# Gated mix of a diagonal state-space layer and a Hedgehog linear attention: loads on one queue, a numerators' factor in four copies, a new step list

## The chip, the cores and the metric

The kernel runs on one core of a Trainium2 chip. The metric is the device time of one execution in microseconds (us), lower is better; the figure for a kernel is the median of several executions.

The engines that matter here: PE (matrix products; its weight loads are listed as PEld), DVE (vector engine), ACT (scalar engine, also activations), POOL (GpSimd) and SP, which issues DMAs. ACT issues DMAs too, in line with its other work; these rows carry the name ACTq, those of SP the name SPq. Each engine takes its own instructions in the order in which the program lists them, and waits at the first whose inputs are not there.

## What is computed

With x of 2048 rows by 512 columns in bf16, the reference is a gated sum of two branches:

```python
g = sigmoid((x * gate_w).sum(-1, keepdims=True))
# branch a: diagonal complex state space
h = Lam_bar * h + B_bar @ x[t]           # for t in 0..2047, 512 complex states
a = 2.0 * real(C @ h) + x * Dskip
# branch b: linear attention, 32 heads of 16
q, k, v = split(x @ wqkv)
phi(y) = concat(softmax(y @ w_phi), softmax(-(y @ w_phi)))
num = phi(q) @ (phi(k).T @ v);  den = phi(q) @ phi(k).sum(0) + 1e-6
b = (num / den) @ wo
out = g * a + (1 - g) * b
```

## The kernel before, in words

**Tiles.** x is cut into 16 tiles of 128 rows. Tile `ti` holds rows of one residue modulo 4 (`ti // 4` is the residue); `x_load` (L224) brings it in by one DMA transpose, so that `xT` holds x with the columns on the partitions. The keys and values are worked on in the order of the tiles, queries and outputs in the order `order` (L259): residues 3, 1, 0, 2.

**Start.** ACT issues the two halves of the key weights into `wk_nat` (L161; the trace calls this buffer C2r), SP the small `w_phi` (L162) and then the transposes of x tiles 0 to 7 (L232). PE runs a row of products that only keep it busy (`F:n`, L802, tile `spin`). `st_W` (L263) transposes a quarter of the key weights on PE, and the copy out of PSUM (`evac`, L113: L115 on ACT, L117 on DVE when the step has `:D`) fills `WTk` (in the trace: Xq). `fold` (L397) multiplies it by the block diagonal of `w_phi`, and the copy fills `Wk2` (in the trace: Wk). From then on `st_k` (L446) makes the projected keys of a tile and `st_v` (L453) its values, four products each (L444) and one copy to SBUF. `st_V` (L299) transposes the state-space parameters on PE and copies them to `vec` (L303); `st_U`, `st_P`, `st_P2` to `st_P4` and `st_i` (L315 to L427) make powers, angles and the tables of sines and cosines out of them, on DVE and ACT.

**Middle.** For a group of two or four tiles `feat_max`, `feat_min`, `feat_exp`, `feat_sum` (L485 to L533) make the two softmaxes: a maximum and a minimum by a tree of DVE operations (L480), two differences (L490, L496), exponentials on ACT (L134), sums by a tree, then a normalising product on DVE (L517 for keys, L528 for the tiles whose features are transposed). `st_a` adds the keys' products with the values into PSUM. `st_p`, `st_g`, `st_z`, `st_h` and `st_K` are the state space in blocks of four time steps: input products, the scan (L616), and the products that bring the states back.

**End.** For a group of four output tiles the normalised query features are transposed by DMA (`phT`, L532). `st_o` (L729) multiplies them by the keys' sums (`pn`, L740), takes the logarithm of the denominators (`ld`) and copies the numerators (`nu`), makes the reciprocal factor `rd` on ACT (L746) and the product `on` on DVE (L748), and transposes it by DMA into `oT` (L753). `st_y` (L708) has put the state-space branch into PSUM; `st_t` (L756) adds `oT` times `wo` (L760), scales by the gate (`ot`, L764 on ACT, L766 on DVE) and writes the tile out (L768).

**What sets the order.** Every piece of work is a generator, and `ORDER` (L24) is a list of tokens. Each token runs one piece of one generator up to its next `yield`; `@3` names the PSUM banks that it takes, `:D` puts a copy on DVE, `:A` an output on ACT's DMA queue. The schedule of PE, DVE, ACT and SP is exactly this order (`manual_schedule`, L150). Tokens of interest: `l8` to `l15` load x tiles, `LV` (L295) loads V's weights, `NR` and `NI` (L275) load the real and imaginary part of B as it lies, `R0` to `R3` and `I0` to `I3` (L279) load B transposed, `O` loads `wo`. A DMA gets one of eight completion semaphores in turn, and waits at its issue for the transfer that had that semaphore before. So `LV` on ACT waits for the first BrT transpose on SP.

The three lines that read the numerators' factor:

```python
aexp(out=rd[:], in_=ld[:], func=ACT.Exp, scale=-1.0, bias=nge[:, ti:ti + 1])
VT(out=on[:]..., in0=nu[:]...,
   in1=rd[:].rearrange("p a h -> p (a h)").unsqueeze(2).to_broadcast([P, 32, Dh]), op=ALU.mult)
```

Of the kernel before, what the change touches and what calls it, by code (L numbers as in the profile page):

```python
# [23 lines left out]
ORDER = """  # L24
B R0 R3 R2 F:40 l8 W0@0 W1@1 W1:D W2@2 W2:D l9 W3@3 W3:D f1@4 W0 f0@5 f0:D LV f2@6 f1 f3@0 f3:D f2 k0@1 k0 NR V@2 V U
P k1@3 U U U P P2 P2 P2 NI k3@4 P R1 P2 P2 P4 k1 P4 k2@5 P4 i3 i3 P2 i3 i3 i0 P3 i0 P3 F:6 V2@6 V2 i3 v3@0 v3 n0 i2
k5@1 k5 k2 i0 k3 i0:D M n0 n0 i1 v4@2 v4 k6@3 k6 n0 l12 l11 v7@6 x0 x0 x0 i1 i1 x0 x0 x1 k4@0 v5@1 k4 i0 i2 i2 i1:D i1
i2:D k7@5 v0@4 p0:D p0:D p0 p0 p1:D p1:D v1@2 v2@3 F:6 n0 x1 x1 x1 k7 i2 x1 x2 v9@0 x2 x2 n1 v5 n1 x2 L p1 l10 v2 e0
I3 n1 n1 e0 n1 v1 v6@5 v0 gw p0:D v6 g100@1 p0:D n2 n2 s0 p1 p1:D v8@7 l15 s0 s0 s0 g000@3 v7 k8@2 l13 D g000 n2 l14
e1 s0 s0 Q0 e1 s0 s1 k8 p0 s1 s1 k9@4 k10@5 p1 g000 g100 g100 k9 k10 a0@62 a0 v9 v10@3 s1 s1 s1 x2 v8 k11@1 p2 k11 n2  # L30
I2 n2 s1 k13@4 k13 g010@5 g010 e2 e2 e2 p1 e2 a1 a1 x3 x3 I0 k12@0 x3 x3 x3 v10 k14@7 I1 k15@1 g011@4 k14 g001@3
g101@7 n3 p0 k15 n3 n3 k12 n3 n3 g001 s2 s2 s2 s2 v11@1 x4 x4 x4 n4 n4 n4 p1 p2 e3 Q1 e3 g001 s2 s2 s2 g011 p3 g011 e3
n4 p3 p3 g101 p2 e3 s3 v11 Q2 g011 g010 g010 g110@0 g110 Q3 w3@3 a2 a2 a2 w1@1 s3 w1 p3 a2 p2 g101 w0@4 w0 g111@5 g111
g111 C0 s3 s3 x4 s3 C5 z0 s3 p3 g110 g111 g110 w2@1 z0 z0 p3 g200@7 g200 w2 w3 q2@4 q3@5 x4 n4 e4 e4 q2 C6 p3 z0 s3
q0@0 q0 z1 g200 g300@1 z1 z1 z1 C4 z1 e4 e4 s4 p2 p2 s4 v14@3 v14 g300 g300 g211@4 z1 z1 c02 q1@0 q1 v15@7 p3 c02 p2
z0 v12@3 z0 z0 s4 g301@1 q15@0 q3 C2 c02 C3 q15 c11 c11 a3 g201@5 c11 v13@0 v13 z1 a3 v12 v15 a3 a3 c13 p2 g210@0 s4
s4 s4 C7 c13 xA z1 c00 q5@3 g201 g201 q5 g311@7 nA z1 s4 z0 z0 g210 c01 c01 c01 xA xA z0 c12 c12 c12 g210 g210 c13
g211 g211 g211 z2 g301 q14@5 xA g301 h00@3 z2 h00 g310@0 C1 h01@4 nA nA q14 c00 g311 g311 c03 c03 h11@1 g311 q9@5 g310
g310 a4 a4 a4 a4 xA nA c03 c00 nA z2 z2 q8@3 c10 c10 r1 h11 q9 eA c10 q10@7 Y z2 eA eA eA r1 Y q8 z2 g310 z2 q4@5 h01
q10 q6@1 sA sA z3 z3 q12@6 h10@3 G q7@4 sA sA z3 q7 q4 q12 sA K3@0 z2 K3 y3@7 sA K2@4 z2 z3 z2 h21@5 y2@6 sA sA O  # L40
q13@0 q13 h10 sA Y Y q6 h20@3 K1@2 K1 r0 r0 z3 K0@0 z3 z3 z3 sA K0 z3 z3 h31@1 h30@2 b0 sA sA h20 h30 h31 h21 y2 y2
END X1 X1 N1 N1 N1 N1 o3@0 X1 o1@3 o2@5 X1 X1 o1 o3 o3@2 o3 o3 q11@1 o3 o2 o2@3 y3 q11 y6@0 o1@2 y0@5 N1 b1 o2 b1 o1
o1 G X2 X2 o2 o1 y3 y6 N2 E1 G G o2 N2 E1 E1 y1@1 E1 o3 o0@3 X2 o0 y0 K2 y7@2 y7 N2 y1 S1 S1 S1 o1 o0@3 o0 X2 S1 X2 y0
o2 y7 t3 S1 o0 o0 r3 S1 r3 y1 o0 S1 N2 N2 t3 t3 t1 S1 t1 E2 E2 b3 y6 b0 y5@4 r2 y5 r2 t2 y4@3 y4 y4 t2 S1 y5 S1 S1 E2
t0 t0 y14@7 E2 S1 b3 b2 y10@1 X3 b2 y10 X3 X3 X3 o5@6 o5 o5@5 o5 o5 y14 o6@6 X3 o6 o6@5 S2 o5 o5 S2 y14 S2 S2 o6 o6 o6
N3 N3 o4@6 o4 o4@5 o4 o4 y10 o7@6 y8@5 y8 S2 S2 o7 o7@6 o4 N3 y8 N3 S2 t0 o7 y11@6 S2 o6 o7 N3 E3 t6 o7 t6:D t5 o4 t4
E3 E3 E3 y11 t5:D t4:D S2 o8@0 o8 o8@4 o8:D o8 y15@3 S2 y15 S3 o9@4 o9 S2 o7 o8 S2 S3 S3 o9@0 o9 o9 y15 S3 o10@4 o9
t4:A o10:D o10@0 o8 o10 o9 S3 t7 o10 y9@0 y9 t7 y13@4 S3 S3 o10 y9 o10 o11@2 S3 S3 S3 t8 S3 o11 o11@2 o11:D o11 o11 t9
y12@2 y12 t8 t8:A t1:A t9:D t9:A o12@5 o12 o12@0 y11 o12:D o12 o12 o11 t2:A t6:A o13@5 o13:D t7:A o13@0 o13:D o13 t10
o13 o14@5 o14:D y13 o14@0 S3 o14:D o14 t11 o14 t10 o12 o13 o15@5 o15:D o15@0 o14 o15:D o15 o15 y12 t12 t12 y13 t13  # L50
t11:D t11:A t12:A o15 t10 t5 t14 t15 t13 t14 t14 t15 t13 t15:A
"""
# [14 lines left out]
def kernel(  # L67
# [65 lines left out]
    def aexp(**kw):  # L133
        ins = nc.scalar.activation(**kw)  # L134
# [159 lines left out]

    def st_LV():  # L295
        nc.scalar.dma_start(out=Wv[:], in_=B_wqkv[:, 2 * D:3 * D].rearrange("(k p) n -> p k n", p=P))
# [432 lines left out]
    def st_o(n):  # L729
        ti = order[n]  # L730
        op_ = pools["op"][1]
        ph = phT0[:, n] if n < 4 else live["ph", n // 4][:, n % 4]
# [15 lines left out]
        VT(out=on[:].rearrange("p g h e -> p (g h) e"), in0=nu[:].rearrange("p a h e -> p (a h) e"),  # L748
           in1=rd[:].rearrange("p a h -> p (a h)").unsqueeze(2).to_broadcast([P, 32, Dh]), op=ALU.mult)
# [3 lines left out]
        nc.sync.dma_start_transpose(out=oT[:], in_=on[:].rearrange("p g h e -> p (g h e)"))  # L753
# [84 lines left out]
```

## Time and profile before

| what | value |
|---|---|
| median of 3 executions | 187.26 us (186.46 to 188.04) |
| the profiled execution, its own time | 188.37 us |
| its span, first to last instruction | 186.6 us |
| mean granted clock of PE over the span | 0.982 |
| DVE, ACT busy | 151.8 us, 126.8 us |
| bytes moved by DMA | 16.99 MB |

A row of a timeline gives start and length in us, the engine, the line, the operation, the tile written and the tiles read, and in brackets the idle time before it and who ended that. A row of the groups gives a count, the total and the mean duration in ns. For a DMA the row is the issue on its queue; the landing time is listed apart.

### The profile page before, as it was taken

What the parts mean: (1) busy time and instruction counts of PE and PEld (TensorE: products, weight loads), DVE (VectorE), ACT (ScalarE), POOL (GpSimd) and SP (SyncE); (2) the same over time, 40 slices, a digit from 0 to 9 for tenths busy, and PEclk for the clock granted to TensorE, in tenths of its full rate; (3) what the DMA queues carried; (4) which work ended last, traced back from release to release, by engine and by line L of the source; (5) the groups of instructions that cost most, each with busy time, mean ns of one, the idle gap of its engine ahead of it and who ended that gap; (6) DMA issues with size and microseconds to landing.
All of it is one profiled execution on the core that took longest, in us unless ns stands there. A gap on an engine that the chain in (4) does not pass through costs nothing. (4 is left out here: it accounts for less than half of the span.)

```text
span 186.6 us, 2958 instructions
## 1 busy us (share of the span) xinstructions
PE 158.2 (85%) x1049; PEld 78.9 (42%) x1068; DVE 151.8 (81%) x306; ACT 126.8 (68%) x258; POOL 9.9 (5%) x28
## 2 busy tenths in 40 slices
...
GB/s 146 112 111 185 171 182 2 84 84 111 77 99 0 11 89 101 56 39 100 62 2 4 0 0 167 59 31 28 28 97 179 86 104 168 107 100 233 174 168 85
DMA packets 55198, 16.99 MB, mean 91 GB/s; under 512 B 50576, under 2 KB 55184, under 8 KB 55184
## 3 DMA queue, kind: packets, MB, share of 16 engines
...
q8 instruction: 8, 0.13, 0.3%
q14 instruction: 6, 0.05, 0.1%
...
## 5 line engine op out<-in xcount | busy, mean ns | idle before, releaser
L444 PEld LDWEIGHTS <-xT 128*128 128x128 bf16 x192 | 18.6, 99 | 32.3 <-issue 12.9
L444 PE MATMUL pk<-Wk,xT 128*128 128x512 bf16 x62 | 17.3, 410 | 9.0 <-ACT Wk L115 7.0
L134 ACT ACTIVATE EEk<-EEk 128x1024 bf16<-128x1024 bf16 x20 | 20.1, 1055 | 0.5 <-DVE EEk L496 0.5
L760 PE MATMUL py<-Wo,oT 128*128 128x512 bf16 x62 | 15.7, 379 | 2.8 <-DMA oT<-on 2.7
L583 PE MATMUL pgq<-xT,LBT 128*128 128x512 bf16 x62 | 16.2, 379 | 0.1
L444 PE MATMUL pq<-Wq,xT 128*128 128x512 bf16 x62 | 15.6, 379 | 0.6 <-ACT Wq L115 0.2
L444 PE MATMUL pv<-Wv,xT 128*128 128x512 bf16 x63 | 15.7, 379 | 0.1
L134 ACT ACTIVATE EEq<-EEq 128x1024 bf16<-128x1024 bf16 x12 | 11.9, 1045 | 4.0 <-DVE EEq L496 4.0
L134 ACT ACTIVATE ld<-pn 128x16 f32<-128x16 f32 x32 | 5.9, 189 | 12.2 <-PE pn L740 11.5
L717 PE MATMUL py<-Wk,H 128*128 128x512 bf16 x32 | 12.1, 378 | 0.9 <-ACT nu L115 0.6
L717 PE MATMUL py<-C2r,H 128*128 128x512 bf16 x32 | 12.1, 379 | 0.2
L718 PE MATMUL py<-Wv,H 128*128 128x512 bf16 x30 | 11.3, 378 | 1.0 <-DVE Wv L679 1.0
L115 ACT CAST Xq<-pq 128x512 bf16<-128x512 f32 x16 | 9.0, 591 | 3.9 <-PE pq L444 3.9
L748 DVE TENSOR_TENSOR on<-nu,rd 128x512 bf16<-128x512 bf16 x16 | 10.9, 684 | 0.5
L718 PE MATMUL py<-C2i,H 128*128 128x512 bf16 x29 | 11.0, 379 | 0.0
L740 PE MATMUL pn<-KVm,phT 128*128 128x68 bf16 x128 | 7.4, 195 | 4.1 <-DMA phT<-EEq 3.3
L740 PEld LDWEIGHTS <-phT 128*128 128x128 bf16 x128 | 6.1, 97 | 10.5 <-DMA phT<-EEq 6.6
L117 DVE CAST nu<-pn 128x256 bf16<-128x256 f32 x10 | 4.1, 422 | 7.9 <-ACT ld L134 7.9
L717 PEld LDWEIGHTS <-H 128*128 128x128 bf16 x64 | 6.2, 98 | 8.3 <-issue 2.1
L115 ACT CAST Xq<-pk 128x512 bf16<-128x512 f32 x16 | 9.0, 600 | 1.1 <-PE pk L444 1.1
L764 ACT ACTIVATE ot<-py,G 128x512 bf16<-128x512 f32 x11 | 7.3, 675 | 3.4 <-PE py L760 3.4
L616 DVE TENSOR_TENSOR_SCAN w<-ssm_par,ut 128x512 bf16<-128x512 f32 x8 | 9.5, 1214 | 0.0
(180 smaller groups left out, 357.1 us busy)
## 6 DMA issues: line engine op xcount, KB each, us to landing
...
Wv<-in_B_wqkv_dram ACTq DMA_DIRECT2D x1, 512.0 KB, 4.5
Bn_r<-in_A_B_re_dram ACTq DMA_DIRECT2D x1, 512.0 KB, 6.9
Bn_i<-in_A_B_im_dram ACTq DMA_DIRECT2D x1, 512.0 KB, 5.2
Wo<-in_B_wo_dram SPq DMA_DIRECT2D x1, 512.0 KB, 4.0
xT<-in_A_x_dram SPq DMA_TRANSPOSE x16, 3.2
```

Source lines behind the costliest of these rows:

```text
L115: nc.scalar.copy(out=out_ap, in_=in_ap)
L117: nc.vector.tensor_copy(out=out_ap, in_=in_ap)
L134: ins = nc.scalar.activation(**kw)
L444: MM(out=pt[:], lhsT=xT[:, kt, ti * P:(ti + 1) * P], rhs=W[:, kt, :], start=(kt == 0), stop=(kt == KT - 1))
L583: MM(out=pgq[:], lhsT=LBT_[:, kt, js], rhs=xT[:, kt, (r1 - 1) * NC:r1 * NC], start=False, stop=(r1 == 1 and kt == KT - 1))
L616: nc.vector.tensor_tensor_scan(out=w[:, ri, :], data0=rb, data1=ut[:, ri, :], initial=0.0, op0=ALU.mult, op1=ALU.add)
L717: MM(out=py[:], lhsT=src[:, j, 0, off:off + P], rhs=cr[:, j, :], start=(j == 0), stop=False)
L718: MM(out=py[:], lhsT=src[:, j, 1, off:off + P], rhs=ci[:, j, :], start=False, stop=False)
L740: MM(out=pn[:, 4 * m:4 * m + 4, :].rearrange("p h e -> p (h e)"), lhsT=ph[:, 4 * hf + m, :], rhs=KVm[:, 4 * hf + m, :], start=(m == 0), st ...
L748: VT(out=on[:].rearrange("p g h e -> p (g h) e"), in0=nu[:].rearrange("p a h e -> p (a h) e"), in1=rd[:].rearrange("p a h -> p (a h)").uns ...
L760: MM(out=py[:], lhsT=oT[:, g, :], rhs=Wo[:, g, :], start=False, stop=(g == HG - 1))
L764: nc.scalar.mul(out=ot[:], in_=py[:], mul=G[:, ti:ti + 1])
```

## The change

The diff does four things. The loads of V's weights, `Bn_r` and `Bn_i` move from ACT's DMA queue to SP's; V's is issued behind the first four x tiles instead of at a token. The factor `rd` is written four times over, side by side, so that the product reads it in runs of four (before, each value is read with a step of 0 over 16). The list `ORDER` is written anew, and the tokens `LV` are gone; its makers counted the time from one operation of an engine to a dependent one of the same engine. The fills are 36, 6 and 6 instead of 40, 6 and 6.

```diff
-    for ti in range(8):
+    for ti in range(4):
+        x_load(ti)
+    nc.sync.dma_start(out=Wv[:], in_=B_wqkv[:, 2 * D:3 * D].rearrange("(k p) n -> p k n", p=P))
+    for ti in range(4, 8):
         x_load(ti)
...
     def st_N(ri):
-        nc.scalar.dma_start(out=(Bn_r, Bn_i)[ri][:], in_=(A_B_re, A_B_im)[ri].rearrange("(j p) d -> p j d", p=P))
+        nc.sync.dma_start(out=(Bn_r, Bn_i)[ri][:], in_=(A_B_re, A_B_im)[ri].rearrange("(j p) d -> p j d", p=P))
...
-    def st_LV():
-        nc.scalar.dma_start(out=Wv[:], in_=B_wqkv[:, 2 * D:3 * D].rearrange("(k p) n -> p k n", p=P))
-        yield
...
-        rd = op_.tile([P, 2, 16], BF16, name="rd")
+        rd = op_.tile([P, 32, 4], BF16, name="rd")
...
-        aexp(out=rd[:], in_=ld[:], func=ACT.Exp, scale=-1.0, bias=nge[:, ti:ti + 1])
-        yield
-        VT(out=on[:].rearrange("p g h e -> p (g h) e"), in0=nu[:].rearrange("p a h e -> p (a h) e"),
-           in1=rd[:].rearrange("p a h -> p (a h)").unsqueeze(2).to_broadcast([P, 32, Dh]), op=ALU.mult)
+        aexp(out=rd[:], in_=ld[:].rearrange("p a h -> p (a h)").unsqueeze(2).to_broadcast([P, 32, 4]), func=ACT.Exp, scale=-1.0, bias=nge[:, ti:ti + 1])
+        yield
+        VT(out=on[:].rearrange("p g h (a b) -> p (g h) a b", b=4), in0=nu[:].rearrange("p c h (a b) -> p (c h) a b", b=4),
+           in1=rd[:].unsqueeze(2).to_broadcast([P, 32, Dh // 4, 4]), op=ALU.mult)
```

The list's first and last tokens, old and new (the whole list is 27 lines):

```diff
-B R0 R3 R2 F:40 l8 W0@0 W1@1 W1:D W2@2 W2:D l9 W3@3 W3:D f1@4 W0 f0@5 f0:D LV f2@6 f1 f3@0 f3:D f2 k0@1 k0 NR V@2 V U
-P k1@3 U U U P P2 P2 P2 NI k3@4 P R1 P2 P2 P4 k1 P4 k2@5 P4 i3 i3 P2 i3 i3 i0 P3 i0 P3 F:6 V2@6 V2 i3 v3@0 v3 n0 i2
+NR F:36 W1@0 W0@1 W0 B F:6 l10 W3@2 W2@3 W1 f0@4 f0 l15 W3:D f3@5 f3 W2:D f1@6 f1:D f2@1 f2 V@2 V P U P P2 P2 NI l9 U
+l8 P P2 P2 k1@0 U R1 k1 P2 P4 l12 U V2@3 P4 k2@4 V2 P2 k2 P4 P3 P3 i0 i2 k0@5 k0 i0 i2 i3 l11 k3@6 k3 i2 R0 n0 v2@1 i0
...
-o13 o14@5 o14:D y13 o14@0 S3 o14:D o14 t11 o14 t10 o12 o13 o15@5 o15:D o15@0 o14 o15:D o15 o15 y12 t12 t12 y13 t13
-t11:D t11:A t12:A o15 t10 t5 t14 t15 t13 t14 t14 t15 t13 t15:A
+o13 o14 o15@5 o15 y15@4 o14 o14 o15@3 o15 o15 o15 o15 y15 t8:A t11 t11:D t11 t12 t12 t9 t13 t9:A t13:D t13 t14 t14 y15
+t12 t14:A t15 t15 t15:A
```

In this new order SP issues, after the small load: x0 to x3, V's weights, x4 to x7, Bn_r, x10, x15, Bn_i, x9, x8, a BrT transpose, x12, x11, two of BrT, x13, the last of BrT, x14. ACT's first work after its two loads and the table load is the copies of W0, W1, f0, f3 and f2; DVE copies W3, W2 and f1. Of the nu copies DVE makes 4 (10 before), of the output scalings 3 (5 before), of the Bn scalings 6 (7 before).

More of the change, by code (lines that the diff above doesn't have):

```diff
@@ L24 @@
 ORDER = """
-B R0 R3 R2 F:40 l8 W0@0 W1@1 W1:D W2@2 W2:D l9 W3@3 W3:D f1@4 W0 f0@5 f0:D LV f2@6 f1 f3@0 f3:D f2 k0@1 k0 NR V@2 V U
-P k1@3 U U U P P2 P2 P2 NI k3@4 P R1 P2 P2 P4 k1 P4 k2@5 P4 i3 i3 P2 i3 i3 i0 P3 i0 P3 F:6 V2@6 V2 i3 v3@0 v3 n0 i2
-k5@1 k5 k2 i0 k3 i0:D M n0 n0 i1 v4@2 v4 k6@3 k6 n0 l12 l11 v7@6 x0 x0 x0 i1 i1 x0 x0 x1 k4@0 v5@1 k4 i0 i2 i2 i1:D i1
-i2:D k7@5 v0@4 p0:D p0:D p0 p0 p1:D p1:D v1@2 v2@3 F:6 n0 x1 x1 x1 k7 i2 x1 x2 v9@0 x2 x2 n1 v5 n1 x2 L p1 l10 v2 e0
-I3 n1 n1 e0 n1 v1 v6@5 v0 gw p0:D v6 g100@1 p0:D n2 n2 s0 p1 p1:D v8@7 l15 s0 s0 s0 g000@3 v7 k8@2 l13 D g000 n2 l14
@@ L30 @@
[L30 to L49, printed above, removed]
@@ L50 @@
-o13 o14@5 o14:D y13 o14@0 S3 o14:D o14 t11 o14 t10 o12 o13 o15@5 o15:D o15@0 o14 o15:D o15 o15 y12 t12 t12 y13 t13
-t11:D t11:A t12:A o15 t10 t5 t14 t15 t13 t14 t14 t15 t13 t15:A
+NR F:36 W1@0 W0@1 W0 B F:6 l10 W3@2 W2@3 W1 f0@4 f0 l15 W3:D f3@5 f3 W2:D f1@6 f1:D f2@1 f2 V@2 V P U P P2 P2 NI l9 U
+l8 P P2 P2 k1@0 U R1 k1 P2 P4 l12 U V2@3 P4 k2@4 V2 P2 k2 P4 P3 P3 i0 i2 k0@5 k0 i0 i2 i3 l11 k3@6 k3 i2 R0 n0 v2@1 i0
+i0:D i3 i0 i3 i3 x0 n0 v4@2 k4@0 v4 x0 R2 n0 k6@3 x0 i1 n0 x0 i1 i3 k5@4 k5 i1 l13 v6@5 x0 i1:D i1 v7@6 x1 R3 n0 x1 n1
@@ new lines @@
+x1 gw i2:D M D p1:D l14 x1 v3@2 v1@4 p0:D p0:D k6 n1 p1:D n1 v6 k4 p0 n1 k7@3 i2 L x1 e0 p0 p0:D n1 e0 v3 s0 k7 p1 p1
+v0@5 n2 v1 e1 v0 x2 k8@0 F:6 s0 I1 x2 s0 e1 v7 x2 s0 s0 s0 v5@7 k10@2 k10 k15@3 v5 p0:D n2 k12@4 s1 k9@5 k9 s0 k8
+k11@6 v9@2 n2 k11 s1 k12 x2 s1 n2 a0@75 a0 s1 s1 s1 I2 x2 I0 n2 x3 g100@0 k13@6 v2 k15 p1 p1 s1 k13 e2 x3 g010@4 p1
+g010 e2 e2 e2 I3 g100 x3 k14@1 k14 n3 x3 n3 p0 a1 a1 p3 v9 g000@3 g000 n3 p0 v10@6 g111@1 g100 p2 g001@2 x3 s2 g001 x4
+Q3 Q0 g000 s2 n3 s2 x4 p3 s2 n3 g011@0 g011 g001 p2 p1 s2 Q2 x4 s2 e3 C2 n4 g010 g011 g011 p2 g110@3 g110 Q1 e3 g010
@@ new lines @@
+e3 g101@2 g101 n4 g111 g101 e3 g111 x4 w3@0 s2 w1@4 z0 z0 p3 w2@2 w2 g110 g110 z0 z0 z0 a2 p2 w3 a2 a2 a2 n4 w1 O s3
+v13@2 n4 g111 p3 p3 C3 w0@3 w0 s3 x4 s3 v8@0 z1 z1 s3 v10 v8 p2 p2 z0 v13 v12@4 p3 q2@1 p2 p2 C4 z1 q3@3 v12 n4 z0 z0
+q0@6 q3 q0 q1@0 g200@2 s3 q1 q2 e4 e4 e4 g301@4 nA z1 z1 z1 v11@3 s3 v11 q5@6 p3 g210@0 s3 xA g210 g201@1 z0 e4 s4 z0
+v14@3 g201 g201 nA g200 a3 z1 s4 C5 a3 a3 g200 g210 c02 c11 xA a3 z1 C6 g210 c11 xA s4 g211@1 g211 nA g211 c02 p3 c02
+s4 z1 xA v14 c01 nA c01 z1 xA nA q5 q4@2 v15@0 v15 g211 s4 s4 c12 g301 g300@3 h10@6 g300 s4 z2 z2 g301 h11@0 c12 c12
@@ new lines @@
+h10 g310@1 g300 q7@4 g310 eA eA q10@3 eA g310 C0 q4 z2 z2 eA g310 z2 sA a4 a4 c01 C1 c10 c10 sA a4 a4 q13@6 Y Y q13
+c00 q10 c00 c03 c11 q14@2 c13 q14 q12@1 q12 q9@6 g311@7 g311 sA C7 c13 z2 c00 h11 c03 g311 h00@3 z2 z2 sA sA q11@2 q11
+Y c10 c13 sA sA z2 h00 z2 q8@0 c03 g311 z3 z3 sA sA q8 sA q7 q15@1 z3 h01@2 h01 h20@7 z3 z3 z3 q6@3 q6 h21@0 Y r1 K3@4
+z3 y2@3 z3 r1 K0@2 q9 K1@6 K1 G K0 y6@5 h21 z3 K3 z3 q15 h30@0 h20 sA sA h31@6 END o1@2 h30 X1 o1 o1@4 y4@7 N1 o0@1 X1
+N1 X1 N1 o1 o1 o1 h31 r0 r0 X1 N1 X1 N1 X2 N2 X2 N2 o1 X2 G o2@0 o2 K2@2 K2 o3@4 o3 y7@6 o3@0 o0 o0@2 o0 E1 E1 E1 E1
```

9 lines of the change are left out of this document (8 added, 1 removed).

## Prediction

> **What bounds the kernel now.** I read the page's first part, then the busy time by stretches, the chain, and the timelines of the stretches in which PE or DVE stands still. The first part names no single owner:
>
> ```profile
> PE 158.2 (85%) x1049; PEld 78.9 (42%) x1068; DVE 151.8 (81%) x306; ACT 126.8 (68%) x258; POOL 9.9 (5%) x28
> ```
>
> The stretches tell them apart (columns: stretch, length, then busy us and instructions of PE, PEld, DVE, ACT, POOL, then clock, DMA share, GB/s):
>
> ```profile
> 8.30:15.70 7.40, 0.38 (x2) 0.10 (x1) 0.54 (x1) 0.64 (x2) 0.00 (x0) 0.82 0.44 99
> 15.70:25.00 9.30, 9.08 (x38) 3.81 (x39) 6.24 (x25) 4.49 (x11) 1.89 (x4) 0.78 1.06 214
> 20.14:163.19 143.05, 132.71 (x878) 64.80 (x893) 137.02 (x255) 115.57 (x229) 5.55 (x14) 1.00 0.36 74
> 163.19:186.60 23.41, 14.12 (x95) 6.12 (x93) 8.01 (x15) 7.65 (x23) 0.00 (x0) 1.00 0.73 151
> ```
>
> So there are three parts. From 8.3 to 15.7 nothing computes. From 20.14 (DVE's first angle instruction) to 163.19 (end of DVE's last feature product) DVE is busy 137.0 of 143.05 us: it sets the pace, with PE close behind. The last 23.4 us belong to nobody: a chain of DMA transposes. Each is priced by itself.
>
> **The dead stretch.** Its timeline:
>
> ```profile
> 1.11 4.45 PE L802 MATMUL spin<-fillw 128*128 128x128 bf16 x40 [1.11 <-DVE fillw L153]
> ...
> 1.32 10.45 SPq L225 DMA_TRANSPOSE xT<-in_A_x_dram  x8
> ...
> 5.25 1.40 PEld L266 LDWEIGHTS <-C2r 128*128 128x128 bf16 x16
> ...
> 6.02 0.58 ACT L115 COPY Xq<-ptw 128x512 bf16<-128x512 bf16 x1 [2.84 <-PE ptw L266]
> ...
> 11.81 3.87 SPq L280 DMA_TRANSPOSE BrT<-in_A_B_re_dram  x3
> 14.63 0.39 ACTq L296 DMA_DIRECT2D Wv<-in_B_wqkv_dram  x1
> 15.06 1.07 ACT L115 CAST Wk<-pf 128x512 bf16<-128x512 f32 x2 [8.46 <-DMA BrT<-in_A_B_re_dram]
> 15.70 1.50 PE L444 MATMUL pk<-Wk,xT 128*128 128x512 bf16 x3 [7.02 <-ACT Wk L115]
> ...
> 17.36 0.17 DVE L303 CAST vec<-pvt 128x12 f32<-128x12 bf16 x1 [8.51 <-PE pvt L301]
> ...
> 18.25 0.16 DVE L328 TENSOR_TENSOR ssm_par<-vec,ssm_par 128x8 f32<-128x8 f32 x1
> ...
> 20.14 0.49 DVE L413 TENSOR_SCALAR kk<-iot,ssm_par 128x512 f32<-128x512 f32 x1
> ```
>
> ACT has to issue Wv's load (L296) before it may copy the folded weights out of PSUM (Wk<-pf), and that issue waits 8.46 us for a BrT transpose, which SP could not issue before 11.81. PE waits for Wk, the parameter transpose pvt stands behind PE's products, and DVE waits for pvt.
>
> **The change, part by part. (a) Loads on SP.** ACT keeps only the two loads of Wk's source (C2r), at its very start; nothing that waits for a DMA stands ahead of the weight copies. Four fills fewer run first (4 x 4.45/40 = 0.45 us), so the W transposes start near 4.8. ACT copies W0 and W1 out (2 x 0.58, from about 5.6 to 6.7). PE makes f0 after W3 and W2 and six more fills (0.67), near 6.9, and ACT copies f0, f3 and f2 (3 x 0.54, half of the 1.07 above) from about 7.3 to 9.0. The first x product starts there: 9.0, not 15.70. DVE gets vec while ACT still copies; ACT's exponential of the time step comes behind f2's copy, so L328 stands at 9.0 + 0.25 = 9.25, not 18.25. From there to L413 it is 1.9 us now; the new list puts five more small instructions into it, some 0.4 us: 9.25 + 2.3 = 11.5, not 20.14. DVE's start moves by **8.6 us**. Its next need is k0's copy, for the first minimum, at 11.5 + 2.5 = 14.0 (two L413 and two L417 pieces come first); ACT has the copies of k1, k2 and k0 (0.58 each, the first 0.9 after its products began), one table load (1.28, row below) and three 4-column activations (0.2 to 0.3) before that, about 9.0 + 4.5 = 13.5. That is 0.5 us of cover.
>
> What SP pays (landing times; then, from the chain, what PE takes for four products of one tile):
>
> ```profile
> Wv<-in_B_wqkv_dram ACTq DMA_DIRECT2D x1, 512.0 KB, 4.5
> Bn_r<-in_A_B_re_dram ACTq DMA_DIRECT2D x1, 512.0 KB, 6.9
> Bn_i<-in_A_B_im_dram ACTq DMA_DIRECT2D x1, 512.0 KB, 5.2
> Wo<-in_B_wo_dram SPq DMA_DIRECT2D x1, 512.0 KB, 4.0
> BrT<-in_A_B_re_dram SPq DMA_TRANSPOSE x4, 4.4
> ```
>
> ```profile
> DMA to landing us min/median/max: 2.8/3.2/7.2
> ```
>
> ```profile
> 162.33 0.86 PE py L724 x4
> ```
>
> (the row without a name is that of the x transposes). An x tile takes SP 10.45/8 = 1.31 us, a load 0.39. Wv, fifth on SP, is issued at 1.32 + 4 x 1.31 = 6.6 and lands near 11.1; PE wants it at 9.0 + 4 x 0.86 = 12.4. x4, issued at 7.0, lands at 10.2 with the median, 14.2 with the worst, and is wanted near 13.3: 0 to 0.9 us, I take 0. Bn_r and Bn_i go out at 12.2 and 15.2, land by 19.1 and 20.4, and DVE scales them first near 23. x8, behind all three, lands at 17.0 + 3.2 = 20.2; fifteen products of 0.86 come first on PE, 9.0 + 12.9 = 21.9. The BrT transposes, now behind x8 to x13, land by 26.1 + 4.4 = 30.5 and are wanted after the first key sums, past 33. So every load keeps 1 us or more of cover but x4.
>
> A rule speaks against expecting anything of (a). The Trainium skill ("DMA: Bandwidth & Descriptors", section "Issuing engines are not separate DMA queues") says that loads from all engines run on the same 16 DMA engines, and that spreading the issues saves only the sequencers' issue time. By it alone the move is worth minus 3 x 0.39 = 1.2 us on SP. The 8.46 us row differs: what is lost is no bandwidth but an engine's place in line behind its own load, of which the rule says nothing.
>
> **(b) Numerators.** Now the product reads its factor with a step of 0; then from four copies, so that runs of four lie side by side.
>
> ```profile
> L748 DVE TENSOR_TENSOR on<-nu,rd 128x512 bf16<-128x512 bf16 x16 | 10.9, 684 | 0.5
> L528 DVE TENSOR_TENSOR EEk<-EEk,rhok 128x2048 bf16<-128x2048 bf16 x1 | 1.2, 1221 | 0.0
> L563 DVE TENSOR_TENSOR K0T<-phT 128x512 bf16<-128x512 bf16 x8 | 3.3, 420 | 0.0
> L134 ACT ACTIVATE rd<-ld,nge 128x32 bf16<-128x32 f32 x16 | 5.3, 331 | 0.2
> L134 ACT ACTIVATE rck<-lgk 128x128 bf16<-128x128 f32 x2 | 0.6, 310 | 0.1
> L115 ACT CAST nu<-pn 128x256 bf16<-128x256 f32 x22 | 8.1, 380 | 0.0
> L764 ACT ACTIVATE ot<-py,G 128x512 bf16<-128x512 f32 x11 | 7.3, 675 | 3.4 <-PE py L760 3.4
> L126 ACT ACT_TABLE_LOAD x2 | 2.6, 1283 | 1.9 <-issue 1.9
> ```
>
> ```profile
> 160.23 0.69 DVE L748 TENSOR_TENSOR on<-nu,rd 128x512 bf16<-128x512 bf16 x1
> 160.84 0.42 DVE L117 CAST nu<-pn 128x256 bf16<-128x256 f32 x1
> ```
>
> L528 repeats a factor in runs of four and takes 1221 ns for 2048 elements, 4 times the elements of L748 at 1.8 times its time; a dense product of 512 (L563) takes 420. Ends: 420 and 684; I take 420, since L528 has the new shape. Independent DVE instructions overlap by some 0.08 us (the last two rows start 0.61 apart, and the first takes 0.69), so an `on` holds DVE 0.60 now and 0.34 then. ACT's exponential grows from 32 to 128 columns; rck writes 128 in 310, rd 32 in 331 with a bias. Ends 0 and +0.1, I take +0.07, 1.1 us over 16, off the path except once in the tail.
>
> **(c) The list.** DVE's instructions between the same two marks are the same, apart from: 9 `on` instead of 11 (9 x 0.34 - 11 x 0.60 = -3.5), one nu copy fewer (-0.34), two output scalings fewer (-1.3), one Bn scaling fewer (-0.26), two tiny ones earlier (-0.16). Work: 137.0 - 5.6 = 131.4. ACT takes six nu copies and two scalings over all, 6 x 0.38 + 2 x 0.68 = 3.6, and (b)'s 1.1; it has 60 us idle. What a list costs or gains in waits the trace of before can't show. Ends: none of the 6.0 us that DVE idles in this stretch, or twice them. Going along DVE's new list I find one wait over 1 us: the numerators of o4 to o7 follow a row of ld, nu and rd on ACT and come 1 to 3 us late together. PE waits longer, some 4 us for the first normalised keys, but has 28 us to spare over the span. I keep 6.0. The last feature product then ends at 11.5 + 131.4 + 6.0 = **148.9**, not 163.19.
>
> **(d) The tail.** SP now and the last feature product:
>
> ```profile
> 161.97 1.22 DVE L528 TENSOR_TENSOR EEq<-EEq,rhoq 128x2048 bf16<-128x2048 bf16 x1
> 158.86 6.46 SPq L753 DMA_TRANSPOSE oT<-on  x3
> 165.43 4.89 SPq L532 DMA_TRANSPOSE phT<-EEq  x3
> 170.41 1.24 SPq L753 DMA_TRANSPOSE oT<-on  x1
> 171.74 1.32 SPq L532 DMA_TRANSPOSE phT<-EEq  x1
> 173.16 6.50 SPq L753 DMA_TRANSPOSE oT<-on  x4
> ...
> 183.51 0.34 ACTq L768 DMA_DIRECT2D out_dram<-ot  x1
> ```
>
> Now the first phT waits 2.2 us behind three oT. In the new list one oT and one output precede it, with their inputs ready, so it starts near 149.0. Against that two oT, not one, stand between the third and the fourth phT: 149.0 + 4.89 + 2 x 1.24 to 2 x 1.63 = 156.8. From the fourth phT's issue to the end it is 186.6 - 171.74 = 14.9 us now, by transpose, pn, numerator, transpose, t15, output; nothing in it changes but 0.3. The span is 156.8 + 14.9 = **171.7**, 14.9 less. The profiled execution took 188.37 with its span of 186.6, 1.1 above the median of 187.26; by the same difference the median becomes 187.26 - 14.9 = **172.4**.
>
> **Rivals.** (1) Only the head's gain lasts: the new list stalls DVE and the tail by what the numerators and the tail should save. For: a list is only as good as the costs it was made with, and in-order engines pass on every miss. Against: DVE's load falls. 187.26 - 8.6 = 178.7. (2) Slower: copies and transposes in one queue drain each other. Each of the three loads would then wait for the tiles in flight (3.2) and the next tile for the load: 4.5 + 6.9 + 5.2 + 3 x 3.2 - 1.2 = 25 us on SP, of which x8's cover of 1.7 is taken off: 172.4 + 23.3 = 195.7. It decides from 16.6 us in all, 5.5 a load. For: now the only 512 KB copy among SP's transposes is Wo. Against: the small Wc load stands ahead of x0 on SP, and the eight x issues still run at 1.31 each. (3) The runs of four bring nothing: 9 x 0.26 = 2.3 us of DVE come back, 174.7. (4) The queue is worth its issue time only, as the rule has it: the 8.6 us stay lost, for another wait takes the place of Wv's (C2r landing late, say), and SP pays 1.2: 182.2. Against: C2r's W transposes run at 5.25 now, with C2r landed.
>
> **How the numbers follow.** Forecast (167 to 177) 0.68, rival (1) 0.13, (2) 0.06, (3) 0.04, (4) 0.05, and 0.04 that list, tail and head together give nothing. The low end, 167, is the sum without DVE's 6.0 us of idle time (166.4), rounded up; the high end, 180, takes in twice the idle time (178.4) and rival (1). Outside lie (2), (4) and the 0.04, 0.15 in all, and a little of the forecast. About 1% is what a measurement of this kernel can tell from no change; faster by more than that is all but (2) and the 0.04: 0.90, within 1% 0.03, slower 0.07.
>
> **What would show it.** Right: the Wk copies on ACT end near 9 with no DMA among their releasers; the first L413 near 11.5; DVE busy about 131 us from there to the last L528-form product, which ends near 149; `on` at 420 ns; the fourth last phT issue near 157. Wrong: a PE or ACT wait for xT or Wv before 25 us (rival 2), `on` at 684 (3), DVE idle over 10 us between the marks, or over 23 us behind them (1).

## The result, and the profile after

The changed kernel takes 163.2 us (median of 4 executions, 162.43 to 163.74) against 187.65 for the kernel before in the same runs: a ratio of 0.870, 95% interval 0.864 to 0.876. Measured again with more executions it took 164.31, ratio 0.875 (0.872 to 0.878). Ratios, here and below, are to the kernel before in the same runs and leave disturbed executions out; the medians take in all. The forecast was 172.4, with a range from 167 to 180: the direction was right, the gain was set some 9 us too small, and the time lies outside the range.

The profiled execution took 162.84 us. The first part of its page:

```profile
span 161.1 us, 2953 instructions
...
PE 151.8 (94%) x1045; PEld 77.4 (48%) x1064; DVE 136.4 (85%) x294; ACT 131.2 (81%) x270; POOL 11.5 (7%) x28
```

PE does the same work but for four fills in a shorter span, DVE is busy 15.4 us less, ACT 4.4 more. By stretches (columns as in the prediction), from DVE's first angle instruction to the end of its last feature product, and from there to the end:

```profile
9.76:137.79 128.03, 124.48 (x839) 61.88 (x854) 125.86 (x248) 115.49 (x228) 6.55 (x12) 1.00 0.48 93
137.79:161.10 23.31, 19.07 (x122) 8.96 (x123) 4.96 (x11) 10.21 (x33) 0.00 (x0) 0.99 0.77 154
```

The three parts of the prediction's sum against these: start 9.76 us where 11.5 were forecast (20.14 before); middle 128.0 where 137.4 were forecast (143.05 before); rest 23.3 where 22.8 were forecast (23.4 before). The miss of the span is 171.7 - 161.1 = 10.6, and 9.4 of it lie in the middle. A second profile of the changed kernel (changed_again, below) has 10.33, 130.0 and 24.1, so that each of the three scatters by 0.6 to 2 us.

The dead stretch is gone. The timeline of the start (`...` stands for rows left out):

```profile
4.41 0.61 PE L269 MATMUL ptw<-ident,C2r 128*128 128x128 bf16 x8
...
5.06 1.07 ACT L115 COPY Xq<-ptw 128x512 bf16<-128x512 bf16 x2 [1.89 <-PE ptw L269]
...
6.13 1.56 ACT L115 CAST Wk<-pf 128x512 bf16<-128x512 f32 x3
6.56 0.58 SPq L234 DMA_DIRECT2D Wv<-in_B_wqkv_dram  x1
...
7.37 0.16 DVE L302 CAST vec<-pvt 128x12 f32<-128x12 bf16 x1
...
7.83 0.17 DVE L327 TENSOR_TENSOR ssm_par<-vec,ssm_par 128x8 f32<-128x8 f32 x1
...
9.76 1.14 DVE L412 TENSOR_SCALAR kk<-iot,ssm_par 128x512 f32<-128x512 f32 x2
```

The weight copies follow PE and end at 7.69; no DMA stands among what they waited for, and vec is there at 7.5 instead of 17.5. What took the place of the wait is short: two waits on PE, for the x tiles x4 and x8, and one on DVE for the imaginary part of B (idle time in brackets). Every one of them is for a tile or a load that the prediction had given cover or next to no wait.

```profile
12.70 1.04 PE L443 MATMUL pv<-Wv,xT 128*128 128x512 bf16 x4 [0.61 <-DMA xT<-in_A_x_dram]
...
22.54 1.04 PE L443 MATMUL pk<-Wk,xT 128*128 128x512 bf16 x4 [1.03 <-DMA xT<-in_A_x_dram]
```

```profile
21.51 0.35 DVE L560 TENSOR_SCALAR phT<-Bn_i,dgs 128x512 bf16<-128x512 bf16 x1 [0.57 <-DMA Bn_i<-in_A_B_im_dram]
```

**Where the middle's time went.** The difference is in how DVE's neighbours follow each other. First the kernel before, then the changed one, around the same tree of sums (start, length):

```profile
64.14 1.22 DVE L480 TENSOR_TENSOR smk<-EEk 128x2048 bf16<-128x2048 bf16 x1
65.39 1.61 DVE L480 TENSOR_TENSOR smk<-smk 128x1024 bf16<-128x1024 bf16 x3
66.92 0.22 DVE L480 TENSOR_TENSOR mxk<-mxk 128x128 bf16<-128x128 bf16 x1
67.06 0.68 DVE L603 TENSOR_TENSOR mc<-uv,T2c 128x1024 bf16<-128x1024 bf16 x1
```

```profile
51.07 1.22 DVE L479 TENSOR_TENSOR smk<-EEk 128x2048 bf16<-128x2048 bf16 x1
52.21 0.22 DVE L479 TENSOR_TENSOR mnk<-mnk 128x128 bf16<-128x128 bf16 x1
52.34 0.68 DVE L479 TENSOR_TENSOR smk<-smk 128x1024 bf16<-128x1024 bf16 x1
52.95 1.22 DVE L489 TENSOR_TENSOR EEk<-Xq,mxk 128x2048 bf16<-128x2048 bf16 x1
54.08 0.42 DVE L479 TENSOR_TENSOR smk<-smk 128x512 bf16<-128x512 bf16 x1
```

Before, the second step of the tree reads what the first has just written and starts 1.25 us after it, 0.03 after its end. In the changed kernel a step of the tree of minima stands between: it starts 1.14 us after the first step, 0.08 before its end, and the tree's second step overlaps that one in the same way. Every DVE instruction of the trace between the marks was sorted like this, by its start against the end of the one ahead. The columns give us, and for the two kinds of neighbours first their count, then the sum of their gaps (+) or overlaps (-); gaps of 0.08 us and more are other idle time. The middle is the sum of the last four columns:

| kernel (profiled execution) | middle | sum of durations | neighbours that wait (gap near 0.03) | neighbours that overlap | other idle time |
|---|---|---|---|---|---|
| before | 143.05 | 152.0 | 71, +2.4 | 178, -15.0 | 3.6 |
| changed | 128.0 | 145.3 | 4, +0.1 | 236, -19.5 | 2.0 |
| spread_only (below) | 138.2 | 151.3 | 30, +1.1 | 216, -17.3 | 3.2 |
| runs_again (below) | 139.9 | 145.6 | 86, +2.9 | 154, -12.6 | 4.0 |
| three_together (below) | 135.7 | 148.9 | 29, +1.0 | 217, -17.8 | 3.5 |

Each of the 71 reads the tile that the one ahead wrote. Such a dependent neighbour costs 2.4 / 71 = 0.034 us of gap, one that overlaps (nearly always an independent one) saves 15.0 / 178 = 0.084, so a place where an independent instruction comes between is worth 0.118 us. 67 places fewer make 7.9 us.

### The profile page after: what moved, and what is told of

It reads as the page before. It is cut to its first block, busy times and chain, and to the rows that moved or that the text cites. A ratio compares the mean times of both kernels' runs of the same rounds, so it can differ in the third digit from the quotient of the medians.

```text
span 161.1 us, 2953 instructions
## 1 busy us (share of the span) xinstructions
PE 151.8 (94%) x1045; PEld 77.4 (48%) x1064; DVE 136.4 (85%) x294; ACT 131.2 (81%) x270; POOL 11.5 (7%) x28
## 4 chain that ended last, share of the span: by engine, by line
PE 68%; SPq 9%; DMA 8%; DVE 7%; ACT 3%; issue 2%; ACTq 0%; DVEq 0%
PE pq L443 9%; SPq L225 8%; PE pgq L582 8%; PE py L716 8%; PE py L717 7%; PE pgq L579 7%; PE py L759 6%; PE pv L443 4%; DMA Bn_i<-in_A_B_im_dram 3%; PE py L723 3%; PE pn L739 2%; PE kvacc L546 2%; PE pk L685 2%; DMA phT<-EEq 2%; PE pk L686 2%; DMA LBT<-K0T 2%
## 5 line engine op out<-in xcount | busy, mean ns | idle before, releaser
L134 ACT ACTIVATE EEk<-EEk 128x1024 bf16<-128x1024 bf16 x20 | 20.6, 1082 | 0.0
L443 PE MATMUL pk<-Wk,xT 128*128 128x512 bf16 x62 | 14.9, 379 | 1.3 <-DMA xT<-in_A_x_dram 1.2
L443 PE MATMUL pq<-Wq,xT 128*128 128x512 bf16 x63 | 15.1, 379 | 0.1
L134 ACT ACTIVATE ld<-pn 128x16 f32<-128x16 f32 x32 | 6.8, 216 | 7.4 <-PE pn L739 7.2
L747 DVE TENSOR_TENSOR on<-nu,rd 128x512 bf16<-128x512 bf16 x16 | 6.7, 422 | 6.9 <-DMA oT<-on 3.3
L763 ACT ACTIVATE ot<-py,G 128x512 bf16<-128x512 f32 x13 | 8.7, 686 | 3.8 <-PE py L759 2.5
L717 PE MATMUL py<-C2i,H 128*128 128x512 bf16 x31 | 11.7, 379 | 0.1
L115 ACT CAST uv<-pgq 128x512 bf16<-128x512 f32 x16 | 9.4, 586 | 2.6 <-PE pgq L582 2.6
L115 ACT CAST nu<-pn 128x256 bf16<-128x256 f32 x29 | 11.1, 407 | 0.0
L582 PEld LDWEIGHTS <-LBT 128*128 128x128 bf16 x64 | 6.2, 98 | 8.2 <-DMA LBT<-K0T 0.8
L115 ACT CAST vx<-pv 128x512 bf16<-128x512 f32 x16 | 9.6, 609 | 0.0
## 6 DMA issues: line engine op xcount, KB each, us to landing
out_dram<-ot ACTq DMA_DIRECT2D x10, 128.0 KB, 2.6
out_dram<-ot SPq DMA_DIRECT2D x6, 128.0 KB, 2.3
```

Source lines behind the costliest of these rows:

```text
L115: nc.scalar.copy(out=out_ap, in_=in_ap)
L443: MM(out=pt[:], lhsT=xT[:, kt, ti * P:(ti + 1) * P], rhs=W[:, kt, :], start=(kt == 0), stop=(kt == KT - 1))
L582: MM(out=pgq[:], lhsT=LBT_[:, kt, js], rhs=xT[:, kt, (r1 - 1) * NC:r1 * NC], start=False, stop=(r1 == 1 and kt == KT - 1))
L717: MM(out=py[:], lhsT=src[:, j, 1, off:off + P], rhs=ci[:, j, :], start=False, stop=False)
L763: nc.scalar.mul(out=ot[:], in_=py[:], mul=G[:, ti:ti + 1])
```

## The experiments

Theory: the middle's extra 9.4 us are these 67 places, 7.9, and 1.6 of other idle time. Rivals: the neighbours mean nothing, and the list gains by waits of other kinds and by work that went to ACT; or the parts of the change only pay together. Ratios are given with 95% intervals.

**The order of DVE's neighbours.** spread_only is the kernel before with only the list changed: steps of the trees change places with other DVE steps. Two of the 30 tokens that moved:

```diff
-i0:D M n0 n0 i1 v4@2 v4 k6@3 k6 n0 l12 l11 v7@6 x0 x0 x0 i1
+i0:D M n0 i1 n0 v4@2 v4 k6@3 k6 l12 l11 v7@6 x0 n0 x0 x0 i1
```

> The kernel before with the list alone changed, and only so that 43 of the 79 places where a DVE instruction stands directly behind the one whose result it reads get an independent DVE instruction between (steps of the trees for maximum, minimum and sum change places with each other; the same instructions, the same loads and numerators). Theory: such a neighbour starts 0.034 us after the end of the one ahead, an independent one 0.084 us before it, so each place is worth 0.118 us: 43 x 0.118 = 5.1 us less, 182.6 (181.5 to 184). Rival: the new list's extra gain is that of waits that fall away and work that went to ACT, and neighbours matter for nothing: 186.7 to 188.7.

Measured: 182.68 us (181.6 to 184.69), ratio 0.972 (0.969 to 0.974): 5.3 less by the ratio, 4.9 by the medians. Its middle:

```profile
21.05:159.27 138.22, 133.64 (x895) 65.56 (x894) 133.95 (x255) 114.46 (x229) 4.83 (x12) 0.99 0.39 76
```

The same 255 DVE instructions as before in 138.22 for 143.05 us, with 30 dependent neighbours for 71: 41 x 0.118 = 4.8, the 4.83 that are measured. By the table 3.7 of them are gaps and overlaps, the rest shorter durations (0.8) and other idle time (0.4). DVE's busy time falls from 137.02 to 133.95 without an instruction less; 2.3 of these 3.1 us are overlaps, in which two instructions count once. The theory holds, the rival falls.

runs_again goes the other way on the changed kernel: second to fourth step of each tree directly behind the one before.

```diff
-i2 R0 n0 v2@1 i0 i0:D i3 i0 i3 i3 x0 n0 v4@2 k4@0 v4 x0 R2 n0 k6@3 x0 i1 n0 x0
+i2 R0 n0 n0 n0 n0 v2@1 i0 i0:D i3 i0 i3 i3 x0 x0 x0 x0 v4@2 k4@0 v4 R2 k6@3 i1
```

> The changed kernel with the steps of each tree for maximum, minimum and sum put back one behind the other (79 more dependent neighbours on DVE), all else as changed. Theory of the neighbours: 79 x 0.118 = 9.3 us more, less what falls into DVE's 2 us of idle time: 163.2 + 8.3 = 171.5 (169.5 to 173), which is near the 172.4 that was predicted. Rival (waits and ACT's share made the extra gain): no more than 1.5 us, 162 to 165.

Measured: 175.52 (174.4 to 179.16), ratio 0.933 (0.931 to 0.936), 11 to 12 us more than the changed kernel by the ratios.

```profile
9.97:149.91 139.94, 128.46 (x857) 62.38 (x856) 133.00 (x248) 116.78 (x228) 4.82 (x12) 0.99 0.44 85
```

82 more dependent neighbours make 9.7 us; the rest of the 11.9 in the middle is other idle time (4.0 for 2.0) and 0.3 of durations. The other idle time may come from steps that are pulled ahead and delay what they pass, but the second profile of the changed kernel has 4.0 of it too, so that its cause stays open. The way and the mechanism are as expected, the size was set some 3 us too low (8.3 more), and 175.5 lies outside the 169.5 to 173 that were expected.

**The loads.** head_only is the kernel before with the change of the loads alone.

```diff
-    for ti in range(8):
+    for ti in range(4):
         x_load(ti)
+    nc.sync.dma_start(out=Wv[:], in_=B_wqkv[:, 2 * D:3 * D].rearrange("(k p) n -> p k n", p=P))
+    for ti in range(4, 8):
+        x_load(ti)
...
-        nc.scalar.dma_start(out=(Bn_r, Bn_i)[ri][:], in_=(A_B_re, A_B_im)[ri].rearrange("(j p) d -> p j d", p=P))
+        nc.sync.dma_start(out=(Bn_r, Bn_i)[ri][:], in_=(A_B_re, A_B_im)[ri].rearrange("(j p) d -> p j d", p=P))
...
-l9 W3@3 W3:D f1@4 W0 f0@5 f0:D LV f2@6 f1
+l9 W3@3 W3:D f1@4 W0 f0@5 f0:D f2@6 f1
```

> The kernel before with the loads' part alone: V's weight behind four x tiles on SP, both halves of B on SP, the old list and the old numerators. If the head's gain stands by itself, the first angle instruction on DVE comes at 9.8 to 11.5 us instead of 20.1 and all behind it moves up with it: 187.7 - 10.4 to 187.7 - 8.6 = 177.3 to 179.1. If the head only pays with a list that is made for it (other waits, on late tiles of x or of B, take its place), 182 or more.

Measured: 183.28 (182.98 to 183.43), ratio 0.977 (0.975 to 0.979): 4.3 less, half of what the earlier start is worth. DVE's first angle instruction does come at 11.59, but later (first DVE, then SP):

```profile
24.55 0.35 DVE L560 TENSOR_SCALAR phT<-Bn_r,dgs 128x512 bf16<-128x512 bf16 x1 [3.65 <-DMA Bn_r<-in_A_B_re_dram]
26.12 0.35 DVE L560 TENSOR_SCALAR phT<-Bn_i,dgs 128x512 bf16<-128x512 bf16 x1 [1.22 <-DMA Bn_i<-in_A_B_im_dram]
```

```profile
12.92 3.86 SPq L283 DMA_TRANSPOSE BrT<-in_A_B_re_dram  x3
16.83 2.57 SPq L225 DMA_TRANSPOSE xT<-in_A_x_dram  x2
19.45 0.58 SPq L279 DMA_DIRECT2D Bn_r<-in_A_B_re_dram  x1
```

B stands on SP behind three BrT transposes and two x tiles. head_bn_first moves only that (the two tokens are taken out further down):

```diff
-B R0 R3 R2 F:40 l8 W0@0
+B NR NI R0 R3 R2 F:40 l8 W0@0
```

> The kernel of head_only, with the two loads of B moved on SP from behind the first three BrT transposes and two x tiles to ahead of them; nothing else. In head_only DVE started at 11.6 us but then stood 3.65 and 1.22 us for these loads, issued at 19.45 and 20.07. Theory: that is where the head's gain went; issued near 13 they land by 19.5, before DVE wants them at 20.9, so 4.9 us come back: 183.3 - 4.9 = 178.4 (177.5 to 179.5). Rival (the old list loses the head's gain to other engines in any case): 182 to 183.5.

Measured: 178.05 (177.0 to 179.28), ratio 0.951 (0.947 to 0.955). The 4.9 us were there. So the loads' part is worth 9.3 us, of which the earlier start (12.20 for 20.14) makes 7.9, but only with an order of SP's own that has B ahead of the BrT transposes, as the new list has.

lv_early asks whether the queue or the place cost the dead stretch: V's weight stays on ACT, only earlier.

```diff
-    for ti in range(8):
+    for ti in range(4):
         x_load(ti)
+    nc.scalar.dma_start(out=Wv[:], in_=B_wqkv[:, 2 * D:3 * D].rearrange("(k p) n -> p k n", p=P))
+    for ti in range(4, 8):
+        x_load(ti)
...
-l9 W3@3 W3:D f1@4 W0 f0@5 f0:D LV f2@6 f1
+l9 W3@3 W3:D f1@4 W0 f0@5 f0:D f2@6 f1
```

> The kernel before with V's weight still issued by ACT, but at the start, ahead of any wait for a BrT transpose; the loads of B stay on ACT where they were, old list otherwise. Theory of the place in line: the weight copies come at 7.7 instead of 15.1, but now the load of B's real part stands on ACT behind a BrT transpose (landed near 15) with the exponential of the time step behind it: the first angle instruction at 17.5 instead of 20.1, 187.6 - 2.6 = 185 (183.5 to 186). Rival (V's load was the whole of the dead stretch): 11.6 instead of 20.1, 179 or less.

Measured: 184.6 (184.24 to 184.79), ratio 0.985 (0.981 to 0.989). Its ACT:

```profile
7.13 1.07 ACT L115 CAST Wk<-pf 128x512 bf16<-128x512 f32 x2 [0.55 <-PE pf L399]
9.16 0.59 ACT L115 CAST Xq<-pk 128x512 bf16<-128x512 f32 x1 [0.95 <-PE pk L443]
15.49 0.44 ACTq L279 DMA_DIRECT2D Bn_r<-in_A_B_re_dram  x1
15.97 0.20 ACT L134 ACTIVATE ssm_par<-vec 128x4 f32<-128x4 f32 x1 [6.23 <-DMA BrT<-in_A_B_re_dram]
```

The weight copies are early, and then the next load on ACT waits for the same BrT transpose (ACT stands idle 6.23 us), with the exponential of the time step behind it; the first angle instruction comes at 18.11. The wait moved on to the next load in line.

wv_on_act is the changed kernel with `nc.scalar` for `nc.sync` at V's weight alone (L234).

> The changed kernel, with V's weight issued by ACT instead of SP, at the same place in the program; there it waits for no more than the second half of C2r (landed by 4.4 us), and ACT's first copy comes at 5.1. Theory of the place in line (what cost 8.46 us was what ACT's load waited for, not that ACT issued it): no change, 162.4 to 164. Rival (copies belong on SP with the transposes, on two queues they hold each other up): the x tiles land late, 165 or more.

Measured: 164.4 (163.12 to 166.71), ratio 0.874 (0.869 to 0.878), between the answers; so it ran again beside the changed kernel itself.

> The changed kernel itself once more, as the measure for the next one and for fourth_phT_first on the same chip in the same rounds: 162.4 to 164.4.

> The kernel of wv_on_act beside the changed kernel, since 164.4 lay above its 163.2 by about what the runs scatter. Theory of the place in line: within 0.6 us of the changed kernel. Rival (two queues hold each other up): 1 us or more above it.

Measured: changed kernel 164.31 (164.03 to 166.1), V's weight on ACT 163.73 (162.83 to 164.71), ratios 0.875 (0.872 to 0.878) and 0.872 (0.869 to 0.875). No difference that these runs can tell: who issues the load does not matter here, where its issue does not hold up ACT's copies.

**The numerators.** rd4_only has the kernel before with the three lines of the factor as changed; rd1_again the changed kernel with them put back.

```diff
-        rd = op_.tile([P, 2, 16], BF16, name="rd")
+        rd = op_.tile([P, 32, 4], BF16, name="rd")
...
-        aexp(out=rd[:], in_=ld[:], func=ACT.Exp, scale=-1.0, bias=nge[:, ti:ti + 1])
+        aexp(out=rd[:], in_=ld[:].rearrange("p a h -> p (a h)").unsqueeze(2).to_broadcast([P, 32, 4]), func=ACT.Exp, scale=-1.0, bias=nge[:, ti:ti + 1])
...
-           in1=rd[:].rearrange("p a h -> p (a h)").unsqueeze(2).to_broadcast([P, 32, Dh]), op=ALU.mult)
+           in1=rd[:].unsqueeze(2).to_broadcast([P, 32, Dh // 4, 4]), op=ALU.mult)
```

> The kernel before with the numerators' part alone. By the prediction's rows an instruction of the product takes 0.42 us for 0.68; eleven of the sixteen lie before the last feature product on an engine that is nearly always busy there: 11 x 0.26 = 2.9 us less, and one or two more on the chain of the tail, 187.7 - 3.2 = 184.5. Rival: the old list holds DVE there by other engines' work, so the time freed becomes idle time: 187 to 187.7.

> The changed kernel with the numerators put back (32 factors, read with a step of 0); list and loads as changed. The product takes 0.68 for 0.42 us: nine before the last feature product, one or two on the tail's chain: 163.2 + 9 x 0.26 + 0.4 = 165.9 (165 to 167) if DVE sets the pace of the middle, as the prediction has it. Rival: PE (busy 124.5 of the 128.0 us between the marks) sets it by now, and half or less is seen: 163.2 to 164.5.

Measured: rd4_only 185.14 (184.44 to 186.24), ratio 0.986 (0.984 to 0.988), 2.5 to 2.7 less; rd1_again 166.26 (165.18 to 168.19), ratio 0.886 (0.882 to 0.889), 2 to 3 us above the changed kernel. The product in rd4_only and in the changed kernel:

```profile
L748 DVE TENSOR_TENSOR on<-nu,rd 128x512 bf16<-128x512 bf16 x16 | 6.7, 416 | 0.5
```

```profile
L747 DVE TENSOR_TENSOR on<-nu,rd 128x512 bf16<-128x512 bf16 x16 | 6.7, 422 | 6.9 <-DMA oT<-on 3.3
```

So a longer product costs time under both lists: DVE has no slack in the middle (in the changed kernel it is busy all of the 20 us in each of the stretches 65 to 85, 85 to 105 and 105 to 125). That a still faster DVE would pay there is not shown, since PE is busy 124.5 of the 128.0 us.

**Do the parts add up?** three_together is head_bn_first with the factor of rd4_only and the list of spread_only.

> The kernel before with three parts in one: the loads of head_bn_first, the numerators of rd4_only and the list of spread_only. If the parts add up: 178.05 - 2.5 - 4.9 = 170.7 (169.5 to 172). Then the list of the changed kernel is worth another 7.5 us: 26 further dependent neighbours between the marks (26 x 0.118 = 3.1), an earlier start (11.6 to 9.8) and work that goes from DVE to ACT (2.1). Rival (PE sets the pace once DVE is faster, so that the parts hide each other): 173 or more.

Measured: 172.0 (170.93 to 173.53), ratio 0.920 (0.915 to 0.924), 15.3 less than before for a sum of 16.7; by the ratios, 15.1 for 17.2. Nearly: 1.4 to 2.1 us are lost between the parts, and no run shows where. From its span of 169.2 to the changed kernel's 161.1 the traces lead by a start at 9.76 for 11.18 (1.4), durations 145.3 for 148.9 (3.6; among them copies and scalings that went to ACT, and two products behind the mark), 25 dependent neighbours fewer and their overlaps (2.6), other idle time (1.4), and back by 0.9 in the tail.

**The tail.** fourth_phT_first moves one token of the changed kernel's list:

```diff
-t3 S3 S3 S3 o10 o10 o10 o9@6
+t3 S3 S3 S3 S3 o10 o10 o10 o9@6
...
-o13@3 o13 S3 y13
+o13@3 o13 y13
```

> The changed kernel with the fourth transpose of the last features issued directly behind the third, ahead of two transposes of numerators (on SP; nothing else). By the prediction's tail, a chain of transposes that starts with the fourth phT: it is issued 3.6 us earlier (142.0 for 145.65), the two others 1.3 us later, so 160.0 to 161.5 for 163.2. Rival: PE, which works without a pause over 0.3 us from 141.6 to 157.2, sets the end of the tail by its own order, and the earlier transpose is not seen: 162.7 to 163.7, or up to 1.3 more if PE waits for the two delayed ones.

Measured: 164.43 (162.86 to 166.11), ratio 0.874 (0.870 to 0.878): no gain. On SP the fourth phT of the changed kernel, then all four of this one and the numerators behind them:

```profile
145.65 1.26 SPq L531 DMA_TRANSPOSE phT<-EEq  x1
```

```profile
137.90 5.42 SPq L531 DMA_TRANSPOSE phT<-EEq  x4
143.41 10.50 SPq L752 DMA_TRANSPOSE oT<-on  x7
```

On PE the last product with wo of the changed kernel, then of this one, with a wait that is new:

```profile
156.20 1.03 PE L759 MATMUL py<-Wo,oT 128*128 128x512 bf16 x4
```

```profile
147.41 1.04 PE L759 MATMUL py<-Wo,oT 128*128 128x512 bf16 x4 [0.71 <-DMA oT<-on]
...
156.75 1.03 PE L759 MATMUL py<-Wo,oT 128*128 128x512 bf16 x4
```

All four phT are issued by 143.3, and PE's last product comes 0.55 us later than without. In the changed kernel PE is busy 19.07 of the 19.44 us from 137.79 to the end of its last product: it works through its list nearly without a pause. It does wait for the fourth phT, but not for long, in its first profile and in that of changed_again:

```profile
149.69 0.18 PEld L739 LDWEIGHTS <-phT 128*128 128x128 bf16 x4 [0.72 <-DMA phT<-EEq]
149.69 0.30 PE L739 MATMUL pn<-KVm,phT 128*128 128x68 bf16 x4 [0.23 <-ACT rd L134]
```

```profile
153.12 0.30 PE L739 MATMUL pn<-KVm,phT 128*128 128x68 bf16 x4 [1.11 <-DMA phT<-EEq]
```

(The first profile puts PE's 0.23 us down to `rd`, but rd ended at 149.64, when the transpose landed too, and the weight load beside it names phT.) So 0.2 to 1.1 us were to be won, not 3.6, and the delayed oT costs 0.7 in their place.

## Why the prediction was right or wrong

**(a) The head, right.** The cause, the remedy and its order of size are confirmed by head_bn_first (9.3 us, 7.9 of them by the earlier start; 8.6 were forecast). The 1.7 us that the start came earlier still are the copies: the first at 5.06 for 5.6, the last at 7.69 for 9.0, since PE's folds follow the copies more closely than was reckoned (L327 at 7.83 for 9.25), and 0.3 on the way from there to L412. Of these 1.7 us some is scatter: L412 starts at 10.33 in the second profile. The cover of the loads on SP did not hold as forecast: x8 was to have 1.7 us and PE waits 1.03 for it, Bn_i was to land 2.6 us before its need and DVE waits 0.57, and x4, taken as 0, costs PE 0.61. That it was no worse is due to the list, which puts B ahead of the BrT transposes. The prediction took that order from the new list without a price of its own; by head_only and head_bn_first it is half of the loads' part. Rival (2), transposes and copies that drain each other in one queue, gave its sign, a PE wait for xT before 25 us, but not its price: 0.6 and 1.0 us on PE instead of 25 on SP. The three copies landed in 3.9, 4.3 and 4.9 us, and SP went on issuing; the x tiles issued directly behind them landed in 5.5, 4.1 and 4.8 us, for the 3.2 that were taken:

```profile
Wv<-in_B_wqkv_dram SPq DMA_DIRECT2D x1, 512.0 KB, 3.9
Bn_r<-in_A_B_re_dram SPq DMA_DIRECT2D x1, 512.0 KB, 4.3
Bn_i<-in_A_B_im_dram SPq DMA_DIRECT2D x1, 512.0 KB, 4.9
```

```profile
DMA to landing us min/median/max: 2.8/4.1/5.5
```

(the last row is that of the x transposes).

Rival (4), the Trainium skill's rule in "DMA: Bandwidth & Descriptors" ("Issuing engines are not separate DMA queues"), has its due in another way: wv_on_act agrees that the issuing engine by itself is worth nothing (0.872 and 0.875). What the rule does not cover is an in-order engine that waits at the issue: ACT stood idle 8.46 us before, 6.23 in lv_early.

**(b) The numerators, right.** 420 ns were taken, 422 measured, and the gain is seen from both sides (2.5 to 2.7 us off the kernel before, 2 to 3 back on the changed one). Rival (3) falls.

**(c) The list, wrong, and this is the step that failed.** "Work: 137.0 - 5.6 = 131.4" took DVE's busy time as a property of its instructions, and "I keep 6.0" its idle time as a property of the kernel. Measured are 125.86 and 2.2. The instructions lost are those that were named; with them alone the middle would be 137.4. But 71 neighbours of the old list waited for each other: 67 x 0.084 = 5.6 us of lost overlap stood in the busy time, and 67 x 0.034 = 2.3 of gaps in the 6.0 us of idle time. The prediction wrote that the trace of before can't show what a list costs or gains in waits; but the 71 places stand in that trace. It even had the price in hand: it read from two rows that independent DVE instructions overlap by 0.08 us, and used it for `on` alone. Its end "none of the 6.0 us" stood for the best that a list can do, and the range's low end of 167 came from it. Beyond that, other idle time fell from 3.6 to 2.0 (4.0 in the second profile of the changed kernel, so this part scatters). Rival (1), a list that stalls DVE, did not occur.

The Trainium skill ("VectorE: DVE Perf Modes", section "The DRAIN you can't avoid") reports eight copies that took 13.88 us with a semaphore after each as with one after the last alone, and says that the semaphore costs nothing extra there. Here an instruction that needs the result of the one just ahead does cost, 0.118 us each, seen in both directions (spread_only, runs_again); for this kernel the measurement decides. Whether it is the semaphore or the data that holds the instruction, no run here tells apart.

**(d) The tail, right in its number, wrong in its reason.** 22.8 forecast, 23.3 measured. But the chain of transposes from the fourth phT on, which was to set it, is not what sets it: with the fourth phT issued 3.6 us earlier nothing is gained. PE, busy 14.12 of the last 23.41 us before and 19.07 of 23.31 now, sets nearly all of it now, and the fourth phT lands as PE gets there. The even sum is luck, a coincidence of two different limits.
